# Sums of squares in PSUM, and four weight pieces converted beside the gram matrix with GpSimd's help

## The chip, the cores and the metric

The kernel runs on one core of a Trainium2 chip. The metric is the device time of one execution, in microseconds (us). The core has engines that work side by side, each in the order of its own program: TensorE (PE, matmuls, with its weight loads shown apart as PEld), VectorE (DVE), ScalarE (ACT), GpSimd (POOL) and SyncE (SP), which issues the loads and stores. They wait for each other on semaphores.

## The reference

```
qn = q / (norm(q, axis=tokens) + 1e-6);  kn likewise       # q, k, v: 6016 x 256
a  = softmax(kn.T @ qn / tau)                               # 256 x 256
x  = v @ a
h  = x @ w_in;   x = (h * sigmoid(1.702 * h)) @ w_out       # 256 -> 2048 -> 256
h  = x @ w2_in;  out = (max(h,0) + alpha * min(h,0)) @ w2_out
```

The columns of q and k are normed over all 6016 tokens, so the sums of squares of all tokens must be there before the softmax. The output is 6016 x 256 in float32.

## The kernel before, in words

The tokens lie over the 128 partitions, 47 rows of 256 columns in each. The first stage loads q and k in 16 tiles of 1, 3, then eight times 4, five times 2, and 1 rows (QK_PARTS). I count them as tiles 0 to 15. For every tile:
- SP issues two loads, into `qk` (five buffers for tiles 0 to 9) or `qk2` (six buffers for the small tiles 10 to 15);
- PE adds the tile's part to the gram matrix k.T @ q, in two PSUM banks (`emit_gram`);
- ACT squares the tile (`sq`, two buffers), and DVE adds the squares to a running sum `acc` of four slots in SBUF. Tiles 0 and 1 are squared straight into it.

Behind tile 9 the four slots are folded to two, and behind tile 14 to one. Then PE sums over the partitions (`nrm`), and a chain of small steps makes the scales: root on ACT, reciprocal on DVE, a diagonal (`diag`), a matmul that spreads it (`bc`), then the scaled gram matrix `G`, its exponential, its transpose `eT`. PE's program is written out: the gram parts of tiles 0 to 13, then nrm, tile 14, bc, tile 15.

The matmuls of the two feed-forward layers run in a split form: every operand is a pair of a high part and the small rest (hi, lo). The weights come as 64-bit numbers and are converted on the chip, in 16 pieces of 512 columns for the first layer: eight of w_in (ia0 to ia7) and eight of w_out (ob0 to ob7), in the order ia0, ia1, ob0, ia2, ia3, ob1, ob2, ... One piece (class Convert) goes through a load into `raw` (two buffers), `scale` and the copy to hi on ACT, and six steps on DVE: shift, signed (writes `top`, one buffer), power, rest (a product), less (top minus hi), low (the sum of both). Class Converter does these steps one at a time; ACT's parts are put into a list (put_off) and emitted where `scalar_work` is called. In the first stage pieces 0 and 1 (ia0, ia1) are converted: piece 0 ahead of tile 2's squares, piece 1 in halves around tile 3's add.

The attention's product is folded into w_in: `emit_w(g)` multiplies eT with pieces ia(2g) and ia(2g+1), twelve matmuls, and gives the weights `wi` of the first layer. `direct(j)` then takes one eighth of the inner dimension for the first two blocks of 512 tokens; in between DVE converts further pieces, as many steps as fit a budget (`beside`). emit_w(1) stands inside direct(1). Piece ob0 must be ready before direct(1), ob1 before direct(2). At the end of the direct stage the operands of the next blocks and sums of the weights (combine_wi) are made; then come the other blocks in groups of four products (`quartet`), which do not concern the diff.

Of the kernel before, what the change touches and what calls it, by code (L numbers as in the profile page):

```python
# [15 lines left out]
P = 128  # L16
# [38 lines left out]
def attention_then_two_ffns(ctx: ExitStack, tc: tile.TileContext, q, k, vT, tau, w1i, w1o, w2i, w2o, alpha, outT):  # L55
# [19 lines left out]
    wto = ctx.enter_context(tc.tile_pool(name="wto", bufs=1))  # L75
    cv = ctx.enter_context(tc.tile_pool(name="cv", bufs=2))
    dram = ctx.enter_context(tc.tile_pool(name="dram", bufs=1, space=bass.MemoryType.DRAM))
    psh = ctx.enter_context(tc.tile_pool(name="psh", bufs=4, space=bass.MemoryType.PSUM))
    pso = ctx.enter_context(tc.tile_pool(name="pso", bufs=4, space=bass.MemoryType.PSUM))

    alpha_sb = const.tile([P, NT], F32, name="alpha_sb")
# [17 lines left out]
    class Convert:  # L99
# [34 lines left out]

        def rest(self):
            nc.vector.scalar_tensor_tensor(self.p, self.raw[:, :, 0], 2.0**-52, self.p, ALU.mult, ALU.mult)

        def less(self):
            nc.vector.tensor_tensor(self.top, self.top, f32(self.hi), ALU.subtract)  # L139

        def low(self):
            nc.vector.tensor_tensor(self.lo, self.top, self.p, ALU.add)
            self.made = True
            if self.done:
                self.done()
# [78 lines left out]
    with tc.manual_schedule():  # L224
# [30 lines left out]
        nc.gpsimd.memset(ones, 1.0)  # L255
        make_identity(nc, ident)

        idle = psh.tile([P, T], F32, tag="h", name="idle")

        def warm(n):  # L260

            for _ in range(n):
                nc.tensor.matmul(idle[:, :P], ones, ident, start=True, stop=True)
# [19 lines left out]
        with ExitStack() as pre:  # L283
            qkp = pre.enter_context(tc.tile_pool(name="qkp", bufs=4))
            sqp = pre.enter_context(tc.tile_pool(name="sqp", bufs=1))
            acc = sqp.tile([P, 2, SLOTS, C], F32, name="acc")
            gram = [pso.tile([P, T], F32, tag="o", name=f"gram{m}") for m in range(2)]
            tiles = []
            rows = [(sum(QK_PARTS[:i]), n) for i, n in enumerate(QK_PARTS)]

            def emit_gram(i):
                r0, n = rows[i]
                for r in range(n):
                    for m in range(2):
                        nc.tensor.matmul(gram[m][:, :C], tiles[i][:, 1, r, m * P:(m + 1) * P], tiles[i][:, 0, r, :],  # L295
                                         start=(r0 + r == 0), stop=(r0 + r == R - 1))

            last = len(rows) - 1
            fold = max(i for i, n in enumerate(QK_PARTS) if n == SLOTS)
            warm(8)  # L300
            for i, (r0, n) in enumerate(rows):
                if i <= fold:
                    qk = qkp.tile([P, 2, SLOTS, C], F32, tag="qk", name="qk", bufs=5)
                else:
                    qk = qkp.tile([P, 2, 2, C], F32, tag="qk2", name="qk2", bufs=6)
                tiles.append(qk)
                for h, src in ((0, q), (1, k)):
                    nc.sync.dma_start(qk[:, h, :n], src[:, r0 * C:(r0 + n) * C].rearrange("p (r c) -> p r c", c=C))
                if i == 2:
                    nc.sync.dma_start(tau_sb, tau.to_broadcast([P, 1]))  # L310
                    nc.sync.dma_start(alpha_sb, alpha)
                if i in (1, 2):
                    piece = conv.todo.pop(0)
                    piece.load()
                    conv.loaded.append(piece)
                if i < last - 2:
                    emit_gram(i)
                if r0 + n <= SLOTS:
                    nc.scalar.activation(acc[:, :, r0:r0 + n], qk[:, :, :n], AF.Square)
                    conv.steps(6 * i)  # L320
                else:
                    sq = sqp.tile([P, 2, SLOTS, C], F32, tag="sq", name="sq", bufs=2)
                    nc.scalar.activation(sq[:, :, :n], qk[:, :, :n], AF.Square)
                    if i == last:
                        nc.vector.tensor_tensor(acc[:, :, 0], acc[:, :, 0], acc[:, :, 1], ALU.add)
                    nc.vector.tensor_tensor(acc[:, :, :n], acc[:, :, :n], sq[:, :, :n], ALU.add)
                    if i in (2, 3):
                        conv.steps(3)
                    if i == fold:
                        nc.vector.tensor_tensor(acc[:, :, 0:2], acc[:, :, 0:2], acc[:, :, 2:4], ALU.add)  # L330
            load_tokens(0, 0)
            load_tokens(0, 1)
            conv.load()
            high(0)
            low(0)

            emit_gram(last - 2)
            nrm = psh.tile([P, T], F32, tag="h", name="nrm")
            for h in range(2):
                for j in range(2):  # L340
                    nc.tensor.matmul(nrm[:, 2 * h + j:2 * h + j + 1], acc[:, h, 0, j * P:(j + 1) * P], ones[:, 0:1],
                                     start=True, stop=True)
            emit_gram(last - 1)
            rr = sm.tile([P, 4], F32, name="rr")
            nc.scalar.activation(rt, nrm[:, :4], AF.Sqrt, bias=tiny)
            nc.scalar.activation(rs, tiny.to_broadcast([P, 2]), AF.Exp)

            nc.vector.reciprocal(rr, rt)
            nc.vector.tensor_tensor(rr, nrm[:, :4], rr, ALU.mult)
            nc.vector.tensor_tensor(rt, rt, rr, ALU.add)  # L350
            nc.vector.tensor_scalar(rt, rt, 0.5, 1e-6, ALU.mult, ALU.add)
            nc.vector.tensor_scalar_mul(rt[:, 2:], rt[:, 2:], tau_sb)
            nc.vector.reciprocal(rr, rt)

            diag = sm.tile([P, 2, P], F32, name="diag")
            bc = psh.tile([P, T], F32, tag="h", name="bc")
            rq = sm.tile([P, C], F32, name="rq")
            for j in range(2):
                nc.vector.tensor_scalar_mul(diag[:, j], ident, rr[:, j:j + 1])
            for j in range(2):  # L360
                nc.tensor.matmul(bc[:, j * P:(j + 1) * P], ones, diag[:, j], start=True, stop=True)
            nc.scalar.copy(rq, bc[:, :C])
            emit_gram(last)
            high(1)
            low(1)
        wti = ctx.enter_context(tc.tile_pool(name="wti", bufs=1))
        gp = ctx.enter_context(tc.tile_pool(name="gp", bufs=5))
        WI = wti.tile([P, NQ, 2, 7, P], F32R, name="wi")
# [135 lines left out]
        def beside(time, convert=False):  # L504

            scalar_work()
            while True:
                own = bg and bg[0].time <= time and not bg[0].waits()
                more = conv.left() and conv.cost() <= time and not conv.waits()
                if own and not (convert and more):  # L510
                    time -= bg[0].time
                    bg.pop(0).run()
                elif more:
                    time -= conv.step()
                else:
                    return
# [373 lines left out]
```

## Time and profile before

| | |
|---|---|
| three runs | 1054.94, 1055.68, 1057.83 us; median 1055.68 us |
| span of the profiled execution, first to last instruction | 1057.7 us |
| PE busy | 1042.0 us, 99% of the span |
| DVE busy | 825.0 us, 78% |
| ACT busy | 750.3 us, 71% |
| POOL busy | 9.7 us, 1% |
| mean granted clock of TensorE | 0.997 |

The page gives no time for the profiled execution but its span; the slowest of the three runs, 1057.83 us, lies nearest to it. A busy share is a mean over stages that have different limits, so what a change is worth in one stage is read from that stage: from the timeline of its engines and from what each waits for last. In a timeline the brackets behind an instruction hold the idle time of its engine ahead of it and what ended it. Times are counted from the start of the span. [...]

### The profile page before, as it was taken

Reading aid. Unit: us, or ns where it says so; the run is one execution under the profiler, and the core shown is the slowest. Engines: PE = TensorE matmul, PEld = TensorE weight load, DVE = VectorE, ACT = ScalarE, POOL = GpSimd, SP = SyncE. Lnnn points to the kernel's source line nnn. Section 1 sums busy time; section 2 is a strip of 40 time slices with the busy share of each in tenths; the row PEclk is TensorE's granted clock in tenths of the full one; section 3 lists DMA queues with packets and bytes.
Section 4 is the critical chain, followed back from the end, with each engine's and each line's share of the span. In section 5 each row is a group of like instructions: output and inputs, shape, how many; then the busy total and the mean of one; then the engine's idle time right before and its main releaser. Section 6 shows DMA issues by size and latency. Waiting matters only on the chain.

```text
span 1057.7 us, 12569 instructions
## 1 busy us (share of the span) xinstructions
PE 1042.0 (99%) x4636; PEld 868.3 (82%) x4636; DVE 825.0 (78%) x1331; ACT 750.3 (71%) x1255; POOL 9.7 (1%) x25
## 2 busy tenths in 40 slices
PE   7989999999999999999999999999999999999998
PEld 6868887788888878888998888888888888888997
DVE  5877888888888888646746888888888888888776
ACT  5565667777777778667766777777777777767775
POOL 0000000000000000000110000000000000000000
PEclk9999999999999999999999999999999999999999
DMA  9622323113133132101545002001100200200100
GB/s 340 246 61 80 120 60 115 60 55 137 59 133 129 61 132 102 51 1 31 202 156 204 1 1 70 11 1 43 38 1 14 67 1 1 75 1 1 40 1 35
DMA packets 30557, 77.62 MB, mean 73 GB/s; under 512 B 3104, under 2 KB 7712, under 8 KB 30496
## 3 DMA queue, kind: packets, MB, share of 16 engines
q1 hardware_dynamic: 28192, 65.29, 17.9%
q0 software_dynamic: 2304, 11.54, 3.3%
q8 instruction: 36, 0.59, 0.2%
q14 instruction: 25, 0.20, 0.1%
HBM read 52.96 MB, written 23.86 MB: 73 GB/s over the span
## 4 chain that ended last, share of the span: by engine, by line
PE 91%; DVE 3%; ACT 3%; DMA 1%; issue 0%; SPq 0%; DVEq 0%; ACTq 0%
PE ps_o L554 46%; PE ps_h L525 41%; PE gram L295 3%; DMA qk<-in_k 1%; ACT ghi L610 1%; PE pw L490 1%; ACT g L596 1%; ACT s L648 0%; DVE g L585 0%; DVE glo L616 0%; DVE x L425 0%; DVE top L123 0%; DVE sc L472 0%; DVE t L461 0%; DVE top L139 0%
## 5 line engine op out<-in xcount | busy, mean ns | idle before, releaser
L554 PE MATMUL ps_o<-ghi,wo 128*128 128x512 f32 (+1 forms) x1536 | 563.7, 386 | 0.0
L525 PE MATMUL ps_h<-x,wi 128*128 128x512 f32 (+1 forms) x2040 | 554.7, 388 | 2.1 <-ACT s L648 1.1
L525 PEld LDWEIGHTS ps_h<-x,wi 128*128 128x128 f32 x2040 | 381.9, 188 | 82.2 <-ACT s L648 6.0
L554 PEld LDWEIGHTS ps_o<-ghi,wo 128*128 128x128 f32 x1536 | 288.6, 188 | 55.2
L554 PE MATMUL ps_o<-glo,wo 128*128 128x512 f32 (+1 forms) x768 | 296.5, 386 | 0.5 <-DVE glo L614 0.5
L585 DVE TENSOR_TENSOR g<-ps_h,s 128x512 f32<-128x512 f32 (+1 forms) x264 | 178.8, 677 | 87.4 <-PE ps_h L525 51.8
L648 ACT COPY s<-ps_h 128x512 f32<-128x512 f32 (+1 forms) x264 | 152.0, 576 | 89.9 <-PE ps_h L525 88.6
L608 ACT ACTIVATE ghi<-g,sign_sb 128x512 fp32r<-128x512 f32 (+1 forms) x192 | 136.9, 713 | 72.2 <-DVE g L604 70.4
L614 DVE SCALAR_TENSOR_TENSOR glo<-g,sign_sb,ghi 128x512 fp32r<-128x512 f32 (+1 forms) x192 | 141.6, 737 | 44.7 <-ACT ghi L608 38.4
L554 PEld LDWEIGHTS ps_o<-glo,wo 128*128 128x128 f32 x768 | 144.3, 188 | 28.6 <-DVE glo L614 0.9
L616 DVE TENSOR_TENSOR glo<-g,ghi 128x512 fp32r<-128x512 f32 (+1 forms) x192 | 126.3, 675 | 32.2 <-ACT ghi L610 32.2
L600 ACT ACTIVATE g<-g,sign_sb 128x512 f32<-128x512 f32 (+1 forms) x144 | 102.3, 710 | 28.3 <-DVE g L585 28.3
L604 DVE SCALAR_TENSOR_TENSOR g<-g,slope_sb 128x512 f32<-128x512 f32 (+1 forms) x144 | 106.0, 736 | 18.9 <-ACT g L600 18.8
L610 ACT CAST ghi<-g 128x512 fp32r<-128x512 f32 (+1 forms) x192 | 113.2, 611 | 3.5
L596 ACT ACTIVATE g<-g 128x512 f32<-128x512 f32 (+1 forms) x120 | 74.7, 623 | 38.0 <-DVE g L585 37.6
L596 ACT ACTIVATE g<-ps_h 128x512 f32<-128x512 f32 (+1 forms) x72 | 42.2, 587 | 24.6 <-PE ps_h L525 23.8
L295 PE MATMUL gram<-qk 128*128 128x256 f32 x188 | 44.3, 396 | 4.0 <-DMA qk<-in_k 4.0
L295 PEld LDWEIGHTS gram<-qk 128*128 128x128 f32 x188 | 36.9, 199 | 10.6 <-issue 5.5
L604 DVE SCALAR_TENSOR_TENSOR g<-ps_h,slope_sb,g 128x512 f32<-128x512 f32 (+1 forms) x48 | 35.1, 731 | 0.0
L600 ACT ACTIVATE g<-ps_h,sign_sb 128x512 f32<-128x512 f32 (+1 forms) x48 | 32.1, 668 | 0.5 <-PE ps_h L525 0.2
L425 DVE TENSOR_TENSOR x<-t,x 128x512 fp32r<-128x512 f32 (+1 forms) x44 | 29.1, 672 | 2.2 <-ACT x L421 2.2
L421 ACT CAST x<-t 128x512 fp32r<-128x512 f32 (+1 forms) x44 | 26.6, 610 | 4.4 <-DVE t L429 4.4
(93 smaller groups left out, 450.3 us busy)
## 6 DMA issues: line engine op xcount, KB each, us to landing
wi<-w2i POOLq DMA_DIRECT2D x8, 896.0 KB, 4.8
xraw<-in_vT SPq DMA_DIRECT2D x10, 512.0 KB, 5.4
x<-ob SPq DMA_DIRECT2D x20, 256.0 KB, 2.2
xraw<-x SPq DMA_DIRECT2D x10, 512.0 KB, 5.3
out_T<-ob SPq DMA_DIRECT2D x20, 256.0 KB, 2.0
raw<-in_w1i SPq DMA_DIRECT2D x8, 512.0 KB, 3.7
qk<-in_q SPq DMA_DIRECT2D x8, 512.0 KB, 9.9
qk<-in_k SPq DMA_DIRECT2D x8, 512.0 KB, 9.6
```

Of the source, the lines that this page charges most:

```text
L295: nc.tensor.matmul(gram[m][:, :C], tiles[i][:, 1, r, m * P:(m + 1) * P], tiles[i][:, 0, r, :], start=(r0 + r == 0), stop=(r0 + r == R - 1))
L525: nc.tensor.matmul(ps[:, :n], WI[:, wq, a, blk], x[:, b, :n], start=(start and i == 0), stop=(stop and i == 2), skip_group_check=True)
L554: nc.tensor.matmul(acc_ps[c][d][:, :n], WO[:, j, a, f, d * P:(d + 1) * P], (hi, lo)[b][:, :n], start=(start and i == 0), stop=(stop and i ...
L585: nc.vector.tensor_tensor(self.src, ps[:, :self.n], s[:, :self.n], ALU.add)
L596: nc.scalar.activation(self.g, self.src, AF.Gelu_apprx_sigmoid)
L600: nc.scalar.activation(self.g, self.src, AF.Copy, scale=sign_sb[:, self.f])
L604: nc.vector.scalar_tensor_tensor(self.g, self.src, slope_sb[:, self.f], self.g, ALU.mult, ALU.max)
L608: nc.scalar.activation(self.hi, self.g, AF.Copy, scale=sign_sb[:, self.f])
L610: nc.scalar.copy(self.hi, self.g)
L614: nc.vector.scalar_tensor_tensor(self.lo, self.g, sign_sb[:, self.f], f32(self.hi), ALU.mult, ALU.subtract)
L616: nc.vector.tensor_tensor(self.lo, self.g, f32(self.hi), ALU.subtract)
L648: nc.scalar.copy(s[:, :n], ps[:, :n])
```

## The change

The running sum of the squares moves to PSUM (`acc_ps`, four banks), and only the add of tile 9 writes it back to `acc` in SBUF. The tile `idle`, `nrm` and `bc` therefore share a pool with the gram matrix, and the pool `psh` opens behind the first stage. Four pieces instead of two are loaded and converted in the first stage, behind tiles 1, 2, 4 and 6. All of a piece is emitted behind an add of DVE: ACT makes scale and the new product r (raw times a constant), DVE shift, signed and power, ACT the copy to hi, and GpSimd three instructions in place of DVE's last three: r times p, top minus hi, and their sum. `r` has one buffer; `qk2` has five instead of six.

```diff
+        def part(self, pool):
+            self.r = pool.tile([P, PIECE], F32, tag="r", name="r", bufs=1)
+            nc.scalar.activation(self.r, self.raw[:, :, 0], AF.Copy, scale=2.0**-52)
+
+        def beside(self):
+
+            nc.gpsimd.tensor_tensor(self.p, self.r, self.p, ALU.mult)
+            nc.gpsimd.tensor_tensor(self.top, self.top, f32(self.hi), ALU.subtract)
+            nc.gpsimd.tensor_tensor(self.lo, self.top, self.p, ALU.add)
+            self.made = True
...
+            psa = pre.enter_context(tc.tile_pool(name="psa", bufs=1, space=bass.MemoryType.PSUM))
+            acc_ps = psa.tile([P, SLOTS, 2, C], F32, name="acc_ps").rearrange("p s h c -> p h s c")
...
-                    qk = qkp.tile([P, 2, 2, C], F32, tag="qk2", name="qk2", bufs=6)
+                    qk = qkp.tile([P, 2, 2, C], F32, tag="qk2", name="qk2", bufs=5)
...
-                if i in (1, 2):
+                if i in (1, 2, 4, 6):
                     piece = conv.todo.pop(0)
                     piece.load()
-                    conv.loaded.append(piece)
+                    pieces.append(piece)
...
                 if r0 + n <= SLOTS:
-                    nc.scalar.activation(acc[:, :, r0:r0 + n], qk[:, :, :n], AF.Square)
-                    conv.steps(6 * i)
+                    nc.scalar.activation(acc_ps[:, :, r0:r0 + n], qk[:, :, :n], AF.Square)
                 else:
...
-                    nc.vector.tensor_tensor(acc[:, :, :n], acc[:, :, :n], sq[:, :, :n], ALU.add)
-                    if i in (2, 3):
-                        conv.steps(3)
+                    if i <= fold:
+                        nc.vector.tensor_tensor((acc if i == fold else acc_ps)[:, :, :n], acc_ps[:, :, :n], sq[:, :, :n], ALU.add)
+                    else:
+                        nc.vector.tensor_tensor(acc[:, :, :n], acc[:, :, :n], sq[:, :, :n], ALU.add)
+                    while pieces:
+                        x = pieces.pop(0)
+                        x.scale()
+                        x.part(sqp)
+                        for step in (x.shift, x.signed, scalar_work, x.power, x.beside):
+                            step()
...
-            nrm = psh.tile([P, T], F32, tag="h", name="nrm")
+            nrm = pso.tile([P, T], F32, tag="o", name="nrm")
...
+        psh = ctx.enter_context(tc.tile_pool(name="psh", bufs=4, space=bass.MemoryType.PSUM))
```

DVE's program of the first stage before, from piece 0 to the add of tile 4 (the sq of a row is that tile's squares: sq_193 of tile 2, sq_215 of tile 3, sq_233 of tile 4; p_166 is piece 0, p_196 piece 1):

```order
L119 TENSOR_SCALAR p_166<-p_166 128x512
L123 SCALAR_TENSOR_TENSOR top_169<-raw_157,p_166 128x512
L133 TENSOR_SCALAR p_166<-top_169 128x512
L136 SCALAR_TENSOR_TENSOR p_166<-raw_157,p_166 128x512
L139 TENSOR_TENSOR top_169<-top_169,wi_hi_171 128x512
L142 TENSOR_TENSOR wi_lo_172<-top_169,p_166 128x512
L326 TENSOR_TENSOR acc_137<-acc_137,sq_193 128x2048
L119 TENSOR_SCALAR p_196<-p_196 128x512
L123 SCALAR_TENSOR_TENSOR top_199<-raw_183,p_196 128x512
L133 TENSOR_SCALAR p_196<-top_199 128x512
L326 TENSOR_TENSOR acc_137<-acc_137,sq_215 128x2048
```

The same place now, from the add of tile 2 (sq_182) to that of tile 5 (sq_266); p_185, p_199 and p_243 are pieces 0, 1 and 2:

```order
L339 TENSOR_TENSOR acc_ps_137<-acc_ps_137,sq_182 128x2x4x256
L118 TENSOR_SCALAR p_185<-p_185 128x512
L122 SCALAR_TENSOR_TENSOR top_190<-raw_158,p_185 128x512
L132 TENSOR_SCALAR p_185<-top_190 128x512
L118 TENSOR_SCALAR p_199<-p_199 128x512
L122 SCALAR_TENSOR_TENSOR top_204<-raw_172,p_199 128x512
L132 TENSOR_SCALAR p_199<-top_204 128x512
L339 TENSOR_TENSOR acc_ps_137<-acc_ps_137,sq_224 128x2x4x256
L339 TENSOR_TENSOR acc_ps_137<-acc_ps_137,sq_240 128x2x4x256
L118 TENSOR_SCALAR p_243<-p_243 128x512
L122 SCALAR_TENSOR_TENSOR top_248<-raw_230,p_243 128x512
L339 TENSOR_TENSOR acc_ps_137<-acc_ps_137,sq_266 128x2x4x256
```

Both pieces of the beginning now stand between the adds of tiles 2 and 3, with three steps each, and piece 2 between those of tiles 4 and 5; piece 3 (not shown) stands likewise between tiles 6 and 7.

ACT's program before, from piece 0's scale to the squares of tile 4:

```order
L116 ACTIVATE p_166<-raw_157 128x512
L129 CAST wi_hi_171<-top_169 128x512
L323 ACTIVATE sq_193<-qk_178 128x2048
L116 ACTIVATE p_196<-raw_183 128x512
L323 ACTIVATE sq_215<-qk_204 128x2048
L129 CAST wi_hi_201<-top_199 128x512
L323 ACTIVATE sq_233<-qk_222 128x2048
```

And now, from the squares of tile 2 to piece 2's copy to hi (wo_74 is the tile that holds the converted w_out):

```order
L335 ACTIVATE sq_182<-qk_167 128x2048
L115 ACTIVATE p_185<-raw_158 128x512
L139 ACTIVATE r_187<-raw_158 128x512
L128 CAST wi_hi_192<-top_190 128x512
L115 ACTIVATE p_199<-raw_172 128x512
L139 ACTIVATE r_201<-raw_172 128x512
L128 CAST wi_hi_206<-top_204 128x512
L335 ACTIVATE sq_224<-qk_213 128x2048
L335 ACTIVATE sq_240<-qk_227 128x2048
L115 ACTIVATE p_243<-raw_230 128x512
L139 ACTIVATE r_245<-raw_230 128x512
L128 CAST wo_74<-top_248 128x512
```

The copy of piece 1 to hi stood behind the squares of tile 3 and now stands ahead of them; the next row behind the last one shown is the squares of tile 5, so piece 2's copy is ahead of them too.

SP's program now, from the loads of tile 4 (qk_227) to those of tile 6 (qk_269); before, the row of raw_230 was not there:

```order
L321 DMA qk_227<-in_q 128x1024
L321 DMA qk_227<-in_k 128x1024
L110 DMA raw_230<-in_w1o 128x1024
L321 DMA qk_255<-in_q 128x1024
L321 DMA qk_255<-in_k 128x1024
L321 DMA qk_269<-in_q 128x1024
L321 DMA qk_269<-in_k 128x1024
L110 DMA raw_272<-in_w1i 128x1024
```

The loads of pieces 2 and 3 stand ahead of tiles 5 and 7 in the one queue that issues them all.

## Rows read from the trace of the kernel before

**Rows 1.** Chain of waits, 0 to 200 us: start, duration, engine, tile, line, count.

```profile
17.58 32.83 PE gram L295 x144
...
79.94 1.28 PE ps_h L525 x3
81.22 1.15 PE ps_o L554 x3
...
102.82 2.78 PE pw L490 x12
```

**Rows 2.** Timeline of PE and PEld: start, duration, engine, line, operation, out<-in, shape.

```profile
50.25 0.95 PE L341 MATMUL nrm<-ones,acc 128*128 128x1 f32 x8
51.06 1.97 PE L295 MATMUL gram<-qk 128*128 128x256 f32 x8
53.30 0.71 PE L361 MATMUL bc<-diag,ones 128*128 128x128 f32 x4 [0.27 <-DVE diag L359]
...
73.55 0.19 PEld L490 LDWEIGHTS pw<-wi_hi,eT_hi 128*128 128x128 f32 x1
...
77.29 0.50 PE L490 MATMUL pw<-wi_lo,eT_hi 128*128 128x512 f32 x1 [2.32 <-DVE wi_lo L142]
...
160.72 0.30 PEld L525 LDWEIGHTS ps_h<-x,wi 128*128 128x128 f32 x2 [1.01 <-ACT wi L475]
```

**Rows 3.** Timeline of DVE, 10 to 68 us.

```profile
13.26 2.29 DVE L326 TENSOR_TENSOR acc<-acc,sq 128x2048 f32<-128x2048 f32 x1 [0.47 <-ACT sq L323]
...
19.47 2.29 DVE L326 TENSOR_TENSOR acc<-acc,sq 128x2048 f32<-128x2048 f32 x1 [2.24 <-ACT sq L323]
...
23.61 7.08 DVE L326 TENSOR_TENSOR acc<-acc,sq 128x2048 f32<-128x2048 f32 x3
...
37.91 1.23 DVE L330 TENSOR_TENSOR acc<-acc 128x1024 f32<-128x1024 f32 x1
...
46.61 0.69 DVE L326 TENSOR_TENSOR acc<-acc,sq 128x512 f32<-128x512 f32 x1
...
67.47 0.68 DVE L142 TENSOR_TENSOR wo<-top,p 128x512 fp32r<-128x512 f32 x1
```

**Rows 4.** Groups by line and shape, 0 to 60 us: count, busy us, mean ns, idle before.

```profile
L326 DVE TENSOR_TENSOR acc<-acc,sq 128x2048 f32<-128x2048 f32 x8 | 18.3, 2292 | 3.2 <-ACT sq L323 2.7
L323 ACT ACTIVATE sq<-qk 128x2048 f32<-128x2048 f32 x8 | 15.3, 1912 | 6.0 <-DMA qk<-in_k 3.2 <-DVE acc L326 2.8
...
L123 DVE SCALAR_TENSOR_TENSOR top<-raw,p 128x512 uint32<-128x512 uint32 x2 | 1.4, 692 | 0.1
...
L129 ACT CAST wi_hi<-top 128x512 fp32r<-128x512 f32 x2 | 1.2, 610 | 1.2 <-DVE top L123 1.2
...
L119 DVE TENSOR_SCALAR p<-p 128x512 uint32<-128x512 uint32 x2 | 0.9, 427 | 9.2 <-ACT p L116 9.1
```

**Rows 5.** Timeline of GpSimd (POOL), 0 to 3 us.

```profile
0.77 0.20 POOL L255 MEMSET ones<- 128x128 f32 x1
...
1.19 0.29 POOL masks.py:199 TENSOR_SCALAR_AFFINE_SELECT ident<-ident 128x128 f32<-128x128 f32 x1
```

**Rows 6.** Groups by line on the page: an add from PSUM, one from SBUF.

```profile
L585 DVE TENSOR_TENSOR g<-ps_h,s 128x512 f32<-128x512 f32 (+1 forms) x264 | 178.8, 677 | 87.4 <-PE ps_h L525 51.8
...
L425 DVE TENSOR_TENSOR x<-t,x 128x512 fp32r<-128x512 f32 (+1 forms) x44 | 29.1, 672 | 2.2 <-ACT x L421 2.2
```

**Rows 7.** SP's issues of loads, timeline: the second load of tile 5.

```profile
13.56 0.33 SPq L308 DMA_DIRECT2D qk<-in_k  x1
```

**Rows 8.** Windows: busy time by engine, granted clock (PEclk), DMA share, GB/s.

```profile
15.10:17.20 2.10, 0.00 (x0) 0.00 (x0) 1.97 (x4) 0.48 (x1) 0.00 (x0) 1.00 1.01 414
17.50:20.50 3.00, 2.92 (x7) 2.41 (x8) 1.03 (x1) 2.81 (x3) 0.00 (x0) 0.50 1.03 415
21.00:24.00 3.00, 3.00 (x16) 2.64 (x15) 2.96 (x5) 2.35 (x2) 0.00 (x0) 1.00 1.03 412
...
79.00:81.50 2.50, 2.50 (x8) 1.91 (x7) 1.33 (x3) 1.25 (x2) 0.00 (x0) 0.50 0.03 7
```

More of the change, by code (lines that the diff above doesn't have):

```diff
@@ L77, in attention_then_two_ffns @@
     dram = ctx.enter_context(tc.tile_pool(name="dram", bufs=1, space=bass.MemoryType.DRAM))
-    psh = ctx.enter_context(tc.tile_pool(name="psh", bufs=4, space=bass.MemoryType.PSUM))
     pso = ctx.enter_context(tc.tile_pool(name="pso", bufs=4, space=bass.MemoryType.PSUM))
@@ L256, in attention_then_two_ffns @@
         make_identity(nc, ident)
-        idle = psh.tile([P, T], F32, tag="h", name="idle")
+        idle = pso.tile([P, T], F32, tag="o", name="idle")
         def warm(n):
@@ L300, in attention_then_two_ffns @@
             warm(8)
+            pieces = []
             for i, (r0, n) in enumerate(rows):
@@ L355, in attention_then_two_ffns @@
             diag = sm.tile([P, 2, P], F32, name="diag")
-            bc = psh.tile([P, T], F32, tag="h", name="bc")
+            bc = pso.tile([P, T], F32, tag="o", name="bc")
             rq = sm.tile([P, C], F32, name="rq")
```

## The prediction

> **What bounds the kernel now.** I read the chain of waits first, to see which work ends last in which stage; then, for the stages that the diff touches, the timelines of TensorE (PE) and VectorE (DVE), for what starts when and who waits; then the groups by line, for durations; then the windows with the granted clock. In the chain the reader sees that after the first loads the gram matrix runs as one unbroken block of 144 matmul records from 17.58 to 50.41 [rows 1]: here PE is the bound. DVE works beside it. It adds the squares of q and k, tile after tile, and its last add starts at 46.61 and takes 0.69, so the norms are ready at 47.3 [rows 3]. PE comes to the norm matmuls (nrm) only at 50.25 [rows 2]. DVE thus has 2.95 us to spare, and no more. From nrm on a thin chain of small steps leads over the diagonal (bc at 53.30) to the softmax, and PE is hardly overlapped in it.
>
> The second place is the folding of the second group of weights, emit_w(1). Its twelve matmuls start at 73.55 and PE stops for 2.32 us at 77.29 for the low half of a weight piece which DVE still converts [rows 2]. The next product starts at 79.94; an undisturbed group of twelve takes 2.78 [rows 1]. So the stop costs 79.94 - 73.55 - 2.78 = 3.6 us. The six matmuls behind it take 1.28 + 1.15 = 2.43 us [rows 1], against 6 x 2.78/12 = 1.39 at full speed: another 1.0, because the clock stands at 0.50 from 79.00 to 81.50 [rows 8].
>
> **The change on the path to the norms.** Tiles are counted from 0; the working starts at the end of DVE's first add, 13.26 + 2.29 = 15.55 [rows 3]. Before, piece 0 was converted ahead of that, while the loads were the limit. Now its DVE steps come behind it, and piece 1's behind piece 0's, before the add of tile 3. ACT too is in another order: the copies hi of both pieces stand ahead of the squares of tile 3. Since ACT and DVE each work through their program in order, the two now wait for each other in turn:
> - Shift 0.43, signed 0.69, power 0.43 of piece 0 [rows 4] end at about 17.2 with the hand-overs.
> - top has one buffer, so signed of piece 1 must wait for all three GpSimd instructions of piece 0. No row shows such an instruction. The nearest is the affine select over 128 elements, 0.29; times four for 512 elements this is 1.15. The memset, 0.20, would give 0.8 [rows 5]; twice the select, as there are two operands, 2.3. I take 1.15, the nearest by kind: 3 x 1.15 = 3.45, to about 20.7; the ends give 19.7 and 24.2.
> - Signed 0.69, hi 0.61, then the squares of tile 3, 1.91 [rows 4], with hand-overs: the add of tile 3 starts near 24.05, against 19.47 before [rows 3]. That is +4.6.
> - Between the adds of tiles 3 and 4, DVE did the last three steps of piece 1, 23.61 - 19.47 - 2.29 = 1.85 [rows 3]; these are GpSimd's now: -1.9.
> - Pieces 2 and 3 stand behind tiles 4 and 6. From the end of an add to the start of the next pass shift 0.46, signed 0.72, hi 0.64 and the next squares 1.94 (the durations of rows 4 with 0.03 a hand-over): 3.76 each, of which DVE works 1.6 and waits for ACT. Together +7.5. GpSimd is done with the piece before well ahead of these, and for them costs nothing.
> - The fold and all adds from it on are DVE's own pace, 37.91 to 47.30 [rows 3], and stay.
>
> Sum: 47.3 + 4.6 - 1.9 + 7.5 = 57.5, and PE, which was ready at 50.25, waits 7.2 us (6.2 or 10.7 at the ends for GpSimd). r, the new ACT product of each piece, runs beside DVE's shift and signed and adds nothing.
>
> Reading and writing the sum in PSUM I cost at nothing: an add with a PSUM operand takes 677 ns and one in SBUF 672 [rows 6], 0.005 x 8 adds. Writing to PSUM by DVE is in no row; by the same difference once more it is under 0.1 in all, and nothing in the rows lets me expect a gain. [...]
>
> [...]
>
> **Transfers.** Two more pieces of 512 KB are in the stream of loads, and SP issues in order. Piece 2 needs piece 0's raw buffer, free near 16.8, when DVE has read it for signed. Tile 5's second load, issued before at 13.56 [rows 7], stands behind it and goes at about 17.5, 4 us later. If PE lost all 4 of them it would be at nrm at 54.3 and the norms, at 57.5, would still end last: this costs nothing. Should tiles 3 and 4 land earlier, because fewer transfers run beside them, that gains nothing either, since ACT takes their squares behind hi of piece 1. The last tile now waits for tile 10's buffer, and the tokens' loads stand behind it; they are issued near 47, when ACT has squared tile 10, and asked for only behind ACT's last squares near 55.
>
> **The clock after the wait.** Before, PE stood still from 15.10 to 17.20, then had 0.50 from 17.50 to 20.50 and 1.00 again in 21.00 to 24.00 [rows 8]. [...] I take 3 us at half speed, as in the stretch above, which do the work of 1.5: +1.2 (0 to 2.5).
>
> **What comes back.** Pieces ob0 and ia2 are ready before the first FFN product. emit_w(1) needs only ia3, which is now first in DVE's line and which takes ob0's place, whose last step ended at 67.47 + 0.68 = 68.15 [rows 3], 5 us before emit_w(1) begins. So 3.6 and 1.0 go. What is late next is ob1, wanted when direct(2) begins; DVE has the time of 60 matmuls (13.6 us) for its 3.6 and for the rest, 4.2. Later PE has no gap until 160.72, where its weight load waits 1.01 for combine_wi(0) [rows 2]. With two pieces fewer that work is done a unit earlier: -1.0 (0 to -1.4).
>
> **Sum:** +7.2 + 1.2 - 3.6 - 1.0 - 1.0 = +2.8 us. The profiled span is 1057.7, and 1057.83, the slowest of the three runs, lies 0.1 above it; the median, 1055.68, is 2 us below. On the span: 1060.5; on the median: 1058.5. The forecast's own range is +0.5 to +6, 1056.2 to 1061.7.
>
> **Rivals.**
> - Faster: the FFN stage is paced by the conversion of pieces far more than PE's gaps show, and the whole chain of the two pieces comes back: for each the six steps of DVE, 2 x 0.43 + 4 x 0.69 = 3.6, and ACT's two, 1.2 by the row of hi [rows 4], together 9.6 in place of 3.6 + 1.0 above. With GpSimd at 0.8 the norms are 6.2 late: 6.2 + 1.2 - 9.6 - 1.0 = -3.2, so 1052.5. It decides once more than 8.4 us return. For it: what PE waits for at 77.29 and 160.72 is DVE's work, or ACT's behind it [rows 2]. Against: between 82 and 160 the chain is PE's own.
> - GpSimd holds back DVE's adds even though their sum lies in PSUM. Each add behind a piece then waits until GpSimd's 3.45 are over instead of 2.1 (hi and squares less power): 3 x 1.35 = +4.0, so 1062.5. No row shows the two at work together. [...]
> - The stop at 77 is replaced by another, as wi_lo's place is taken by ob1's or the sums of a unit: the 4.6 don't come back, +7.4, so 1063.
> - The added transfers make PE late itself: less wait at nrm, the same end; no time of its own.
>
> **How the numbers follow.** Forecast 0.52, faster rival 0.18, GpSimd 0.15, no return 0.15. A difference under 0.3% (3.2 us) can't be told from none. The forecast lies just under that line: of its 0.52, 0.22 slower, 0.28 same, 0.02 faster. The first rival: 0.10 faster, 0.08 same. The other two: 0.28 slower, 0.02 same. Together faster 0.12, same 0.38, slower 0.50. The range 1052 to 1063.5 leaves out a tenth at each end.
>
> **What would show it.** nrm near 57.5 instead of 50.25, with PE idle 7 us or more ahead of it and DVE's last add just before; in DVE's timeline waits for GpSimd near 18 to 21, and for ACT's squares of about 2 us behind the pieces at tiles 4 and 6; a clock of 0.50 behind nrm; no PE wait in the second folding. It is wrong if the norms come before 53, if PE waits ahead of nrm for loads, or if a new PE stop stands between 62 and 90.

## The result and the profile after

| | before | after |
|---|---|---|
| median | 1056.74 us (4 runs, 1054.94 to 1057.83) | 1063.65 us (4 runs, 1063.02 to 1064.06) |
| ratio, 95% interval | | 1.0065 [1.0053, 1.0078] |
| span of the profiled execution | 1057.7 us | 1061.2 us |
| POOL busy | 9.7 us | 25.0 us |

The kernel became 6.9 us slower. The forecast was 1058.5, with a range up to 1063.5: the direction was right, the time lies outside, by 0.15. The difference, +2.8 forecast and +6.9 measured, says more: of the 5.15 by which the time misses the forecast, 1.06 is the base, whose median went from 1055.68 to 1056.74 with a fourth run of 1057.79.

The timeline of PE after (start, duration, what; in brackets the idle time ahead and what ended it) answers to [rows 1, 2]:

```profile
16.25 33.01 PE L307 MATMUL gram<-qk 128*128 128x256 f32 x144 [1.94 <-DMA qk<-in_k]
56.92 1.87 PE L360 MATMUL nrm<-ones,acc 128*128 128x1 f32 x8 [7.66 <-DVE acc L341]
58.65 3.63 PE L307 MATMUL gram<-qk 128*128 128x256 f32 x8
...
71.17 5.15 PE L545 MATMUL ps_h<-x,wi 128*128 128x512 f32 x20
```

The gram matrix ends at 49.26 (16.25 + 33.01), and PE then stands still for 7.66 us until DVE has the norms. Behind the wait the four gram matmuls of tile 14 take 3.63 instead of 1.97 [rows 2]; each float32 matmul here leaves two records in the trace, so they stand as x8. From nrm to the first FFN product (ps_h) it is 71.17 - 56.92 = 14.25; before, that product began at 62.40, 12.15 behind nrm. The granted clock (PEclk, third value from the right) shows why:

```profile
52.00:56.50 4.50, 0.00 (x0) 0.00 (x0) 4.15 (x5) 3.16 (x5) 0.00 (x0) 0.50 0.50 202
57.00:62.00 5.00, 5.00 (x16) 4.37 (x17) 2.63 (x10) 1.75 (x3) 0.00 (x0) 0.50 0.01 2
62.00:66.00 4.00, 3.82 (x29) 3.50 (x28) 2.28 (x5) 1.55 (x4) 0.00 (x0) 1.00 0.02 4
```

It fell to 0.50, half of full speed, while PE was idle and stayed there until 62. Why DVE is late stands in its own timeline, against [rows 3]:

```profile
17.13 0.90 DVE L118 TENSOR_SCALAR p<-p 128x512 uint32<-128x512 uint32 x1 [0.81 <-ACT p L115]
20.54 0.69 DVE L122 SCALAR_TENSOR_TENSOR top<-raw,p 128x512 uint32<-128x512 uint32 x1 [2.50 <-POOL wi_lo L145]
...
23.72 4.71 DVE L339 TENSOR_TENSOR acc_ps<-acc_ps,sq 128x2048 f32<-128x2048 f32 x2 [2.03 <-ACT sq L335]
...
32.03 2.30 DVE L339 TENSOR_TENSOR acc_ps<-acc_ps,sq 128x2048 f32<-128x2048 f32 x1 [2.04 <-ACT sq L335]
...
40.34 4.70 DVE L339 TENSOR_TENSOR acc_ps<-acc_ps,sq 128x2048 f32<-128x2048 f32 x2 [2.04 <-ACT sq L335]
...
56.17 0.69 DVE L341 TENSOR_TENSOR acc<-acc,sq 128x512 f32<-128x512 f32 x1
```

There is one wait of 2.50 for GpSimd, because `top` has one buffer, and three of 2.03 to 2.04 for ACT's squares, which stand behind the copy hi. An add in PSUM takes 2.30, as in SBUF [rows 3]. ACT in its turn had waited for DVE's `top`, and then has two tiles of squares to do:

```profile
21.26 0.62 ACT L128 CAST wi_hi<-top 128x512 fp32r<-128x512 f32 x1 [2.80 <-DVE top L122]
21.79 3.70 ACT L335 ACTIVATE sq<-qk 128x2048 f32<-128x2048 f32 x2
```

GpSimd, the first piece:

```profile
16.48 1.27 POOL L143 TENSOR_TENSOR p<-r,p 128x512 f32<-128x512 f32 x1 [15.00 <-DVE p L132]
17.71 1.45 POOL L144 TENSOR_TENSOR top<-top,wi_hi 128x512 f32<-128x512 f32 x1
19.24 1.26 POOL L145 TENSOR_TENSOR wi_lo<-top,p 128x512 fp32r<-128x512 f32 x1
```

The second folding now has no stop. The chain of waits shows its twelve matmuls whole, and the next folding 4.42 us behind its place before, where it stood at 102.82 [rows 1]:

```profile
82.66 2.79 PE pw L510 x12
107.24 2.78 PE pw L510 x12
```

So far nearly every step of the forecast is there, and on the profiled executions the sum is too: 1061.2 - 1057.7 = +3.5, forecast +2.8. But the medians are 6.9 apart. The executions of after have a time 1.8 us above their span (1063.02 against 1061.2). If that holds before, a span of 1057.7 means 1059.5, more than any run timed so far. My theory was therefore that the profiled execution of before was a long one. The rival was that the base is steady and that the missing 3 us are a cost in after that its trace doesn't show beside before's.

### The profile page after: what moved, and what is told of

Same layout as the page of the kernel before. It is cut to its first block, busy times and chain, and to the rows that moved or that the text cites. A ratio compares the mean times of both kernels' runs of the same rounds, so it can differ in the third digit from the quotient of the medians.

```text
span 1061.2 us, 12586 instructions
## 1 busy us (share of the span) xinstructions
PE 1042.7 (98%) x4636; PEld 870.1 (82%) x4636; DVE 816.4 (77%) x1319; ACT 752.1 (71%) x1259; POOL 25.0 (2%) x37
## 4 chain that ended last, share of the span: by engine, by line
PE 90%; DVE 3%; ACT 3%; DMA 2%; issue 1%; POOL 0%; SPq 0%; DVEq 0%; ACTq 0%; POOLq 0%
PE ps_o L574 47%; PE ps_h L545 42%; DMA qk<-in_q 1%; PE pw L510 1%; ACT sq L335 1%; DMA qk<-in_k 1%; DVE acc L341 1%; ACT ghi L630 1%; ACT g L616 1%; DVE acc_ps L339 0%; ACT s L668 0%; DVE g L605 0%; PE gram L307 0%; DVE acc L339 0%; DVE top L122 0%
## 5 line engine op out<-in xcount | busy, mean ns | idle before, releaser
L339 DVE TENSOR_TENSOR acc_ps<-acc_ps,sq 128x2048 f32<-128x2048 f32 x7 | 16.1, 2300 | 18.9 <-ACT sq L335 18.6
```

## The experiments

They ran in three batches of four, in the order of the table; the first and the third on one chip, the second on another. Before measured 1055.78, 1057.40 and 1056.47 us there. Each ratio is to before in the same batch; as recorded it is not exactly the quotient of the two medians (for after_b that would be 1.0049).

| label | what | median us | ratio to before, 95% interval |
|---|---|---|---|
| before_a | before again | 1055.83 | 0.9998 [0.9989, 1.0008] |
| hi_late | hi and GpSimd's steps behind the next squares, two buffers for top and r | 1052.85 | 0.9975 [0.9964, 0.9985] |
| top2 | two buffers for top | 1060.58 | 1.0046 [1.0031, 1.0061] |
| warm_nrm | 24 idle matmuls ahead of nrm | 1060.83 | 1.0050 [1.0035, 1.0065] |
| after_b | after again | 1062.53 | 1.0057 [1.0042, 1.0072] |
| psum_only | sums in PSUM, pieces as in before | 1056.97 | 1.0000 [0.9987, 1.0013] |
| sbuf_sum | after, sums in SBUF | 1066.20 | 1.0093 [1.0078, 1.0108] |
| warm37 | 37 idle matmuls ahead of nrm | 1061.34 | 1.0039 [1.0023, 1.0056] |
| before_b | before again | 1056.58 | 0.9999 [0.9990, 1.0008] |
| before_warm | before, idle matmuls ahead of tile 3 | 1056.54 | 1.0003 [0.9994, 1.0012] |
| two_pieces | after with two pieces | 1060.99 | 1.0040 [1.0027, 1.0054] |
| hi_late3 | hi_late with three pieces | 1051.98 | 0.9956 [0.9944, 0.9969] |

### The base: before_a, before_b, after_b

No edit in any of the three.

> The kernel before, once more and unchanged, to see whether its profiled execution (span 1057.7 us, norm matmuls at 50.25) is typical of its timed runs. Theory A (a base that varies): the executions after show their time 1.8 us above their span, so a span of 1057.7 would be a time of 1059.5, above all four timed runs (1054.94 to 1057.83). So the profiled execution was a long one: TensorE waited longer for tile 3 and ran slower from 17.50 to 20.50 than it mostly does. Expected: span 1053 to 1056, the big gram block starting or ending 2 to 3 us earlier, norm matmuls at 47.5 to 48.5, where VectorE's last add ends and not TensorE's own work is the bound. Rival B (the base is steady and time and span lie otherwise in this kernel): span 1057 to 1058, norm matmuls at 50.0 to 50.5, time 1056 to 1058.

The span was 1053.1 and the time 1055.29. PE's timeline, and the last add of DVE:

```profile
16.09 31.32 PE L295 MATMUL gram<-qk 128*128 128x256 f32 x144 [1.78 <-DMA qk<-in_k]
47.24 0.95 PE L341 MATMUL nrm<-ones,acc 128*128 128x1 f32 x8
...
59.38 6.79 PE L525 MATMUL ps_h<-x,wi 128*128 128x512 f32 x27
...
74.28 0.51 PE L490 MATMUL pw<-wi_lo,eT_hi 128*128 128x512 f32 x1 [2.32 <-DVE wi_lo L142]
```

```profile
45.57 0.69 DVE L326 TENSOR_TENSOR acc<-acc,sq 128x512 f32<-128x512 f32 x1
```

and the chain and a window of the clock:

```profile
74.28 2.13 PE pw L490 x8
98.22 2.79 PE pw L490 x12
```

```profile
17.50:20.50 3.00, 3.00 (x16) 2.64 (x15) 2.52 (x2) 2.84 (x3) 0.00 (x0) 1.00 1.03 415
```

Theory A holds, but for its last clause: nrm stands 0.3 ahead of its range, and PE's own block is still the bound, for DVE's last add ends at 46.26. Against the profiled execution of [rows 1, 2, 8], tile 3 comes 1.49 earlier (16.09 for 17.58), the 144 records take 1.51 less, since the clock doesn't fall behind the wait, and nrm stands 3.01 earlier. The stop of 2.32 in the second folding is there, but the clock doesn't fall behind that either (1.00 from 74.00 to 77.50): the third folding stands 4.60 earlier, which is 1.58 more. 1.49 + 1.51 + 1.58 = 4.58, the whole difference of the spans (4.6).

> The kernel before once more, for a third trace of it. Its 41 executions so far have spans of 1052.4 to 1056.6 us; those with a mean clock of 1.000 lie at 1052.4 to 1054.5, those at 0.998 mostly above. Theory (half clock comes in some executions only, behind a wait of TensorE): if this trace has a clock of 0.998, one stretch at 0.50 of some 3 us is in it, behind the wait for tile 3 or the stop in emit_w(1), and the span is 1 to 3 us longer than 1053.1; if 1.000, there is none and the span is 1053 to 1054. Rival (the executions differ in loads alone): norms late by what tile 3 is late, without a stretch at 0.50.

This trace had a clock of 0.999, between the two cases named, and a span of 1052.9. Its gram block is as in before_a, with nrm at 46.97 and no stretch at 0.50:

```profile
15.81 31.32 PE L295 MATMUL gram<-qk 128*128 128x256 f32 x144 [1.41 <-DMA qk<-in_k]
46.97 0.95 PE L341 MATMUL nrm<-ones,acc 128*128 128x1 f32 x8
```

So what the theory said of a trace at 0.998 was not put to the test. But the 73 executions of before in the three batches whose spans are known lie at 1052.4 to 1056.9, median 1054.3, with times 1.7 to 2.2 above. The one at 1057.7 from which I forecast is longer than all of them. The two traced ones are among the shorter. Of the 73, 30 have a mean clock of 1.000 or 0.999, as these two, and a median span of 1053.15; 43 have 0.998 or 0.997, and 1054.7. The gap of 1.55 is the size of one stretch at half clock, so the usual execution may have one of the two of [rows 8]; no trace of one shows it.

> The kernel after, once more and unchanged, beside fresh runs of before. It asks what of after's profiled execution (span 1061.2) is typical. In it the last 64 us, with the narrow matmuls of 448 columns, were 1.1 us longer than in both traces of before. If that belongs to this one execution: span near 1060, time 1061.5 to 1062.5, 6 to 7 above before. If it belongs to the change: span 1061 to 1062, time 1063 to 1064, 7.5 to 8.5 above before. In both cases the norm matmuls stand at 56.5 to 57.2, since ScalarE and VectorE set them and not the loads.

The span was 1060.3 (times 1062.09 to 1062.84), 5.1 above before by the medians and 6.0 by the ratio, at or a little under the first case's 6 to 7; nrm as forecast:

```profile
17.06 33.01 PE L307 MATMUL gram<-qk 128*128 128x256 f32 x144 [2.65 <-DMA qk<-in_k]
57.02 1.86 PE L360 MATMUL nrm<-ones,acc 128*128 128x1 f32 x8 [6.96 <-DVE acc L341]
```

This is the other half of the answer. The gram block starts 0.81 later than in the first trace of after, and nrm moves by 0.10: the wait for the norms swallows what the loads and the clock do ahead of it. Before, the same lateness goes to the end: in before_warm (below) tile 3 comes 1.00 later than in before_a, and nrm 1.01 and the third folding 1.00 later. The extra 1.1 us in the last 64 us were that execution's own.

### Where the norms' 9.7 us come from: two_pieces, top2, hi_late

```diff
-                if i in (1, 2, 4, 6):
+                if i in (1, 2):
```

> After with two pieces beside the gram matrix, as before has them, but in after's new order and with its GpSimd steps. It divides after's loss of about 9.7 us at the norms (56.92 against 47.24) between the order of pieces 0 and 1 and the two pieces more. Theory (each further piece costs VectorE 1.6 of work and 2.04 of waiting, 7.4 together): norms at 49 to 50, stop of 2.3 in emit_w(1) still there, time 2 to 3 us above before. Rival (the first two pieces carry most of the loss): norms at 53 or later, time 5 or more above before.

The norms came at 49.89, as the theory said; DVE's six adds from tile 3 on run without a break:

```profile
23.70 14.32 DVE L339 TENSOR_TENSOR acc_ps<-acc_ps,sq 128x2048 f32<-128x2048 f32 x6 [2.04 <-ACT sq L335]
```

```profile
49.89 1.87 PE L360 MATMUL nrm<-ones,acc 128*128 128x1 f32 x8 [2.41 <-DVE acc L341]
51.62 3.76 PE L307 MATMUL gram<-qk 128*128 128x256 f32 x8
...
79.57 0.50 PE L510 MATMUL pw<-wi_lo,eT_hi 128*128 128x512 f32 x1 [2.33 <-DVE wi_lo L152]
```

Pieces 2 and 3 thus cost 56.92 - 49.89 = 7.0 at the norms (forecast 7.5), the new order of pieces 0 and 1, with their steps on GpSimd, the other 49.89 - 47.24 = 2.65. The time was missed: +4.5, not 2 to 3. Behind the wait of 2.41 the half clock is there (0.50 from 50 to 52; from nrm to the first FFN product 64.66 - 49.89 = 14.77). So the order of two pieces alone costs about 5 us at the first FFN product (64.66 against 59.38 in before_a).

```diff
-            self.top = cv.tile([P, PIECE], F32, tag="top", name="top", bufs=1)
+            pool = self.src_pool or cv
+            self.top = pool.tile([P, PIECE], F32, tag="top", name="top", bufs=2 if self.src_pool else 1)
...
+                        x.src_pool = sqp
```

> After, with two buffers for top in the first stage and nothing else. It takes away VectorE's wait of 2.50 us for GpSimd at 20.54 and leaves the three waits for ScalarE. If each wait on this chain counts in full: norm matmuls at 54.4 instead of 56.92, still behind a TensorE wait of about 5 us and with half clock behind it, time 1060.5 to 1061.5. Rival: the add of tile 3 waits for ScalarE's squares anyway, and only 0.5 or less is won: 1063 to 1063.7.

The time was as the theory had it, but nrm came at 55.27, 1.65 earlier and not 2.5. The wait for GpSimd went; DVE's steps then ran beside GpSimd's, and there they are longer, 1.64 and 1.38 for 0.69 and 0.43:

```profile
18.04 1.64 DVE L124 SCALAR_TENSOR_TENSOR top<-raw,p 128x512 uint32<-128x512 uint32 x1
19.72 1.38 DVE L134 TENSOR_SCALAR p<-top 128x512 uint32<-128x512 uint32 x1
22.18 4.70 DVE L341 TENSOR_TENSOR acc_ps<-acc_ps,sq 128x2048 f32<-128x2048 f32 x2 [1.09 <-ACT sq L337]
```

hi_late has these buffers, two for r, and another order (shown without the buffers):

```diff
                     nc.scalar.activation(sq[:, :, :n], qk[:, :, :n], AF.Square)
+                    scalar_work()
+                    while begun:
+                        begun.pop(0).beside()
...
-                        for step in (x.shift, x.signed, scalar_work, x.power, x.beside):
+                        for step in (x.shift, x.signed, x.power):
                             step()
+                        begun.append(x)
```

> After, but with two buffers for top and for the ScalarE product, and with the copy hi and the GpSimd steps of each piece put behind the squares of the next tile, so that ScalarE and VectorE no longer wait for each other in turn. Theory (the wait of 7.66 us ahead of the norm matmuls is the sum of these waits, 2.50 for GpSimd and three of 2.04 for ScalarE): norms at 47 to 49, TensorE reaches the norm matmuls without a wait of over 1 us at 49 to 50.3, no half clock behind it, emit_w(1) without a stop, time 1053 to 1055. Rival (the work itself, eight more ScalarE passes of 0.6 in the stage, paces the norms, and not the order): norms at 53 to 55, time 1059 to 1062.

```profile
31.57 17.50 PE L309 MATMUL gram<-qk 128*128 128x256 f32 x80 [0.26 <-DMA qk<-in_k]
50.37 1.05 PE L367 MATMUL nrm<-ones,acc 128*128 128x1 f32 x8 [1.30 <-DVE acc L346]
51.28 1.97 PE L309 MATMUL gram<-qk 128*128 128x256 f32 x8
```

The order of ACT and DVE, with the buffers that it needs, was the cause: nrm stands 6.55 earlier than in after and the half clock is gone (1.00 from 50 to 66), with the same four pieces and the same instructions, and this is faster than before. Of the 6.55, top's second buffer alone gave 1.65 (top2); r's was not tried alone. The norms missed their range by 1.4, and PE's wait is 1.30, not under 1: in the block PE now waits 1.35 (at 24.13) and 0.26 for loads.

### The clock behind the wait: warm_nrm, warm37, before_warm

```diff
             emit_gram(last - 2)
+            warm(24)
             nrm = pso.tile([P, T], F32, tag="o", name="nrm")
```

> After, with 24 more idle matmuls (128x128, into a tile that nobody reads; some 5.7 us at full clock) between the gram matrix and the norm matmuls, so that TensorE works through most of its wait of 7.66. Theory (behind the wait the half clock costs about 2.1 us: the way from the norm matmuls to the first FFN product took 14.25 us against 12.15 before): norm matmuls still at 56.9, the eight gram matmuls behind them 2.0 instead of 3.63, clock 1.00 from 52 to 62, time 1061 to 1062. Rival (the longer way comes from ScalarE and VectorE, and the clock hardly matters): way of 13.8 or more, time 1063 to 1064.

nrm stood at 56.63, but behind a rest of the wait (3.20), and the clock fell again behind it (1.00 from 52 to 57, a mean of 0.66 from 57 to 62); 13.45 from nrm to the first FFN product, between both theories:

```profile
56.63 1.05 PE L361 MATMUL nrm<-ones,acc 128*128 128x1 f32 x8 [3.20 <-DVE acc L341]
57.55 3.29 PE L307 MATMUL gram<-qk 128*128 128x256 f32 x8
```

So the wait was filled up, with `warm(37)`:

> After, with 37 idle matmuls in place of 24 in the wait ahead of the norm matmuls. With 24, a wait of 3.20 us was left, the clock fell again behind it (the eight gram matmuls took 3.29), and only part of the 2.1 us came back. 37 take some 8.5 us and end at about 56.4. Theory (TensorE's standing still is what costs the clock): wait under 1 us, eight gram matmuls in 2.0, way from the norm matmuls to the first FFN product 12.2, time 1059 to 1060. Rival (the way is long for another reason): way of 13.5 or more, time 1060.5 or more.

```profile
48.96 8.42 PE L273 MATMUL idle<-ident,ones 128*128 128x128 f32 x74
57.22 0.95 PE L361 MATMUL nrm<-ones,acc 128*128 128x1 f32 x8
58.03 1.97 PE L307 MATMUL gram<-qk 128*128 128x256 f32 x8
...
69.42 6.79 PE L546 MATMUL ps_h<-x,wi 128*128 128x512 f32 x27
```

With the same late norms the way is 12.20, as before the change, and the clock is 1.00 from 50 to 66. The half clock costs 14.25 - 12.20 = 2.05 us, and PE's standing still is its cause here. The time, 1061.34, missed its 1059 to 1060 and came only 1.2 below after_b: nrm is 0.2 later, and the profiled execution, the median one, had a last stretch 1.1 longer, as the first of after.

```diff
                 if i < last - 2:
                     emit_gram(i)
+                if i == 2:
+                    warm(6)
```

> Before, with six idle matmuls (1.4 us) behind the gram matmuls of tile 2, so that TensorE doesn't stand still ahead of tile 3. Theory (the half clock behind that wait is one of the two reasons why executions of before differ): no stretch at 0.50 between 15 and 22, norm matmuls at 47 to 48 in the trace, the longest executions gone, median 0.5 to 1.5 below before on the same chip. Rival (the spread comes from the loads or from elsewhere): median within 0.3 of before.

The rival held: 0.1 above before. In its trace there is no half clock up to the end of PE's work (1.00 in every window from 5 to 1052), and the span is 1055.4 all the same, for tile 3 came at 17.09 and the last stretch was long. Of its ten executions six still have a mean clock of 0.998. The half clock behind the wait for tile 3 is thus not what alone spreads the executions of before.

### PSUM and GpSimd: psum_only, sbuf_sum

psum_only is after with the two pieces of before, converted on DVE in before's order (its qk2 keeps five buffers).

> Before, with the sums of squares gathered in PSUM as after has it, and its two pieces converted as before on VectorE. Theory (a sum in PSUM costs and gives nothing; all of the loss is in the conversions): adds of 2.29 to 2.31 us, norm matmuls where before has them, 47 to 48, time within 1 us of before. Rival (the sums in PSUM are slower, or PSUM ties up something else): norms 0.5 us or more later, time 1 us or more above before.

```profile
22.18 9.50 DVE L340 TENSOR_TENSOR acc_ps<-acc_ps,sq 128x2048 f32<-128x2048 f32 x4
```

Four adds took 9.50, in SBUF 9.47 (before_a); ratio 1.0000. The forecast's zero for PSUM was right as a price.

```diff
-                    nc.scalar.activation(acc_ps[:, :, r0:r0 + n], qk[:, :, :n], AF.Square)
+                    nc.scalar.activation(acc[:, :, r0:r0 + n], qk[:, :, :n], AF.Square)
...
-                        nc.vector.tensor_tensor((acc if i == fold else acc_ps)[:, :, :n], acc_ps[:, :, :n], sq[:, :, :n], ALU.add)
+                        nc.vector.tensor_tensor(acc[:, :, :n], acc[:, :, :n], sq[:, :, :n], ALU.add)
```

> After, with the sums of squares kept in SBUF as before has it; the four pieces and their order as in after. It asks whether PSUM shields VectorE's adds from GpSimd. Theory (VectorE's two-input SBUF work and GpSimd's get in each other's way: in after the steps beside GpSimd took 0.90 instead of 0.42): the adds that run beside GpSimd's steps take longer than 2.29, by up to GpSimd's 3.8 a piece, norms 0.5 to 4 us later than 56.9, time 0.5 to 4 us above after. Rival (adds of two inputs are not touched, only the others): adds of 2.29, norms at 56.5 to 57.2, time that of after.

The theory held: the norms came at 61.31, 4.3 later than in after_b (a little over the range), and the time was 3.7 more. DVE's and GpSimd's timelines:

```profile
24.06 6.05 DVE L337 TENSOR_TENSOR acc<-acc,sq 128x2048 f32<-128x2048 f32 x2 [2.03 <-ACT sq L333]
```

```profile
23.41 1.27 POOL L144 TENSOR_TENSOR top<-top,wi_hi 128x512 f32<-128x512 f32 x1
24.76 3.20 POOL L145 TENSOR_TENSOR wi_lo<-top,p 128x512 fp32r<-128x512 f32 x1
```

Two adds take 6.05 instead of 4.71, behind each of three pieces, 3 x 1.34 = 4.0; and GpSimd's sum, 1.27 behind the first piece, takes 3.20 beside them. The two adds are 1.34 longer, about one sum of 1.27, and the sum is 1.94 longer, most of an add; in what way they hold each other up these rows don't show. In after, with the sum in PSUM, both keep their length, 4.71 for two adds and 1.28 for the sum beside them. So PSUM is worth about 4 us here, but only where GpSimd works beside it: without GpSimd's steps (psum_only) it was worth nothing.

### Fewer pieces: hi_late3

```diff
-                if i in (1, 2, 4, 6):
+                if i in (1, 2, 6):
```

> The late hi copies with two buffers, as measured (0.9975 of before), with three pieces instead of four: at tiles 1, 2 and 6. With four the norm matmuls waited 1.30 and the loads were the pace from tile 4 on (TensorE waits of 1.35 and 0.26 for them); a piece is half of a tile's load, some 1.3 us. Theory: norms at 48.5 to 49.3, emit_w(1) still without a stop, since one piece is more than the 2.3 us of it, and 1 us less than with four: ratio 0.996 to 0.997. Rival (the fourth piece is needed): a stop of 1 us or more in the second folding, or later at the weight load near 160, and a time as with four or longer: 0.9975 or more.

```profile
16.33 31.32 PE L309 MATMUL gram<-qk 128*128 128x256 f32 x144 [1.81 <-DMA qk<-in_k]
47.60 1.05 PE L367 MATMUL nrm<-ones,acc 128*128 128x1 f32 x8
```

```profile
72.23 2.78 PE pw L517 x12
96.81 2.79 PE pw L517 x12
```

PE comes to nrm without a wait, the second folding has no stop, and the third stands 1.41 ahead of before_a's. The norms came ahead of the 48.5 to 49.3 expected. The ratio is 0.9956 [0.9944, 0.9969], a little better than expected too: this version beats both kernels, before by 4.5 us. Against hi_late, which ran in another batch, the two intervals overlap.

## Why the prediction was wrong

Its sum, term by term, against the execution from which it was made and against before_a, a short one (span 1053.1, the median is 1054.3):

| term | forecast | after less the profiled before | after less before_a |
|---|---|---|---|
| norms late | +7.2 | 56.92 - 50.25 = +6.7 | 56.92 - 47.24 = +9.7 |
| clock behind nrm | +1.2 | 14.25 - 12.15 = +2.1 | 14.25 - 12.14 = +2.1 |
| second folding | -4.6 | 4.42 - 8.77 = -4.35 | 9.02 - 11.79 = -2.8 |
| the rest | -1.0 | -0.9 | -0.9 |
| sum | +2.8 | +3.5 | +8.1 |

The medians, 6.9 and 5.1 apart, lie between the two columns, as does the median execution of before.

**The step that failed** is the last of the working: "the median, 1055.68, is 2 us below. On the span: 1060.5; on the median: 1058.5". It took the profiled execution to be 2 us long and those 2 us to stand alike in both kernels. It was longer, 3.4 us by the spans (1057.7 to the median of 1054.3). And its length did not carry over: against before_a, 3.0 of it lay ahead of nrm (tile 3 late, then half clock), where after waits for the norms anyway, and 1.6 behind the stop that after removes. A saving and a hiding place had been counted that neither of the two later traces of before has, and that the median execution, 3.4 shorter, cannot have in full. In those traces "PE, which was ready at 50.25" is ready at 47.0 to 47.2, DVE's "2.95 us to spare" are 0.98 (47.24 - 46.26), and the return of "3.6 and 1.0" is worth 2.8. The 0.50 in the two stretches of [rows 8] was on view in the forecast; that it need not be there in each run was not asked.

**The path to the norms** was right: 57.5 forecast, 56.9 and 57.0 measured. The wait for GpSimd ("to about 20.7"): 20.54. The add of tile 3 at 24.05: 23.72. Each further piece 3.76: 3.60 in after (32.03 - 28.43), and 7.0 for two by two_pieces. GpSimd's 1.15 measured 1.27 (1.45 for one of the twelve). The norms were 0.6 early since tile 2's add began at 12.51, not 13.26.

**Tile 5's load** hiding behind the norms: right. Neither trace of after has a PE wait for a load inside the gram block; warm_nrm, the same program up to there, has one of 0.69 at 23.64, and the wait for the norms hides it.

**The clock** was mis-sized: 2.05 to 2.1 by two ways (the traces and warm37), forecast 1.2, its bounds 0 to 2.5. The 1.2 was an estimate, the 1.5 less the 0.27 of bc's wait [rows 2]; no run shows it. The slow stretch was longer than its 3 us: in after the clock is 0.50 from the start of nrm at 56.92 to 62, 5.1 us.

**What comes back**: the stop went and no other took its place. The 3.6 was misread: it runs from a weight load (73.55) to a start in the chain (79.94); by PE's own starts it is 79.74 - 73.77 - 2.78 = 3.2. With the 1.0 that makes 4.2, and 4.35 was measured. The last term agrees by luck: its -0.9 is made of -2.1 between 107 and 570, outside the forecast's 0 to -1.4, and +1.1 in the last stretch of that one execution. Between 107 and 570 the weight load's wait of 1.0 for combine_wi went, as forecast, and of its waits for ACT's s, 4.7 in eight became 3.6 in six, on which the forecast had nothing. So the +3.5 beside +2.8 is in part luck too.

**Rivals.** The faster one is refuted: from the first FFN product to 570 us, 4.9 came back against before_a and 6.4 against the profiled before, under the 8.4 from which it decides. GpSimd holding back adds out of PSUM is refuted by the 2.30 in after, and sbuf_sum shows a cost of that size, 4.0, had the sum stayed in SBUF; but there the adds start no later behind ACT's squares (2.03) and are longer, so the price agrees by luck. No return: refuted. Transfers: no time of their own in after. In hi_late, where the engines no longer wait for each other in turn, ACT waits 1.86 and 1.77 for the loads of tiles 5 and 7, behind pieces 2 and 3; hi_late3, without the piece at tile 4, has its norms 2.8 earlier, of which the load and the conversion were not told apart.

Open: what half clock the executions of before at 0.998 have; why the last 64 us take 1.1 us longer in some executions, of before_warm and warm37 as of after (between two marks of the chain, 980.96 and 1050.09 in before, it is 69.1 in eleven of the fourteen traces and 70.28 in these three, at a granted clock of 1.00); and why the base differs by 1.6 us between the first two batches. Nothing was tried on these.

## What to carry to other kernels

Before a sum is put on one profiled execution, place that execution among the timed ones, and ask of each stretch on which the slack rests (a late load, a stretch at half clock) whether it is there every time; a change that makes another engine last there hides such lateness, so that it may not be subtracted from both sides. Work that is handed to a third engine is only free if the two that hand it over do not wait for each other in their own order: the same instructions made the kernel 5 to 7 us slower or 3 us faster, depending on whether the copy stood ahead of or behind the next squares (with a second buffer for top and r). And convert only as many pieces early as the later stop needs: three did no worse here than four.

## What the runs showed of the hardware

- VectorE's adds with both inputs in SBUF and GpSimd's sum of a piece, also from SBUF, held each other up: adds of 2.30 took 2.8 and 3.2 (6.05 for two), the sum 3.20 instead of 1.27 (sbuf_sum). One-input steps beside GpSimd were longer too, a shift 0.90 instead of 0.42 (after) and a bitwise and 1.38 instead of 0.43 (top2). An add with one operand in PSUM kept its 2.30 (after, at 32.03, beside GpSimd's steps at 31.38 and 32.73).
- What the half clock cost at nrm did not grow with the wait: the way to the first FFN product was 14.77 behind a wait of 2.41, 14.25 behind 7.66 and 14.21 behind 12.92 (sbuf_sum). At a clock of 1.00 it was 12.1 to 12.2 in before_a, before_b and warm37 without a wait and in hi_late behind 1.30, and 12.80 and 13.11 in psum_only and hi_late3, where bc waited 0.9 for DVE.
- At tile 3 the clock fell behind waits of 2.52 (before), 1.94 (after), 1.93 (warm37) and 2.65 (after_b), to means of 0.50 to 0.56 from 17.5 to 20.5, and not behind 1.90 (two_pieces) and 2.43 (sbuf_sum), with 1.00 there. Behind the stop of 2.31 to 2.33 in the second folding it fell in before (0.50 from 79.0 to 81.5) and two_pieces (0.56 from 80 to 82), and not in before_a, before_b and before_warm (1.00 there), nor in psum_only, whose eight matmuls behind the stop took 2.12, as in before_a (2.13): about the same wait of PE costs 1.5 to 1.7 us in one execution and nothing in another.
